# Reading the stationary operands of two attention products 128 columns wide instead of 99

## The chip, the cores and the metric

The kernel runs on one core of one Trainium2 chip. The metric is device time in microseconds (us). Each run also leaves a profile of one execution, the trace. The engines are named as in the profile: PE is TensorE's matmuls, PEld its weight loads (which overlap matmuls), DVE is VectorE, ACT is ScalarE, POOL is GpSimd and SP is SyncE.

## The reference

A layer norm with modulation, an attention block with 8 memory tokens and segments of 32 tokens, and an MLP, on 2048 tokens of width 1024. The part that matters is the attention of 32 heads of 128:

```python
q = jnp.einsum('btd,dhe->bhte', h, Wq)      # and k, v
scores = jnp.einsum('bhqe,bhke->bhqk', q, k) * scale
scores = jnp.where(mask[None, None], scores, -1000000000.0)
p = _softmax(scores, axis=-1)
o = jnp.einsum('bhqk,bhke->bhqe', p, v)
```

## The kernel before

The kernel packs the tokens of a head into 22 tiles: tile 0 has T0 = 104 columns, the others TW = 99 (three segments of 32 and three memory columns). Queries and keys of a head lie transposed, 128 partitions by 2188 columns, tile after tile. A score matmul has the keys of one tile as stationary operand (`lhsT`) and its queries as moving operand (`rhs`). Five tiles (a group) share one PSUM tile, one exponential on ACT and one mask multiply on DVE. An output matmul has the exponentials E as stationary operand and the values with a column of ones as moving operand (129 columns). There are 32 x 22 = 704 of each kind. The program interleaves them with the projections of the next head pair (480 moving columns each).

```python
def col0(t):
    return 0 if t == 0 else T0 + (t - 1) * TW

def scores(h, g):
    QT, KTt = QTs[h % 3], KTs[h % 3]
    rows = T0 if g == 0 else TW
    o = 0
    ps = psS.tile([P, 512], F32, name="ps_s")
    for t in SG[g]:
        w = T0 if t == 0 else TW
        nc.tensor.matmul(ps[:rows, o:o + w], lhsT=KTt[:, col0(t):col0(t) + rows], rhs=QT[:, col0(t):col0(t) + w], start=True, stop=True)
        o += w
    E = ep.tile([P, 512], BF16, name="E")
    # ... exponential on ACT, mask multiply on DVE, both on [:rows, 0:o]

def outs(h, j):
    V, O = Vs[h % 2], Os[h % 2]
    ts = VG[j]                                   # three tiles
    n, rows = len(ts), T0 if j == 0 else TW
    ps = psO.tile([P, 3, DH + 1], F32, name="ps_o")
    for i, t in enumerate(ts):
        k = T0 if t == 0 else TW
        nc.tensor.matmul(ps[:rows, i, :], lhsT=state["e", h, t // 5][:k, col0(t) - col0(t // 5 * 5):col0(t) - col0(t // 5 * 5) + rows], rhs=V[:k, t, 0:DH + 1], start=True, stop=True)
    # ... reciprocal and scaling on DVE or ACT
```

Of the kernel before, what the change touches and what calls it, by code (L numbers as in the profile page):

```python
# [9 lines left out]
BF16 = mybir.dt.bfloat16  # L10
# [9 lines left out]
P = 128  # L20
S = 2048
D = 1024
KT = D // P
H = 32
DH = 128
# [23 lines left out]
QW = T0 + (NT - 1) * TW + 5  # L49
# [11 lines left out]
def kernel(ctx, tc, A_x, A_mem0, A_Wq, A_Wk, A_Wv, A_Wo, A_seg_len, B_x, B_w1, B_w2, B_w3, B_w4, c, w_mod, out,  # L61
           dbg=None, force_fallback=False, no_fallback=False):
    nc = tc.nc
# [103 lines left out]
    def first_pass(late_hook):  # L167
# [55 lines left out]
        LQ = ExitStack()  # L223
        qkp = LQ.enter_context(tc.tile_pool(name="up_qk", bufs=1))
        QTs = [qkp.tile([P, QW], BF16, name=f"QT{i}") for i in range(3)]
        KTs = [qkp.tile([P, QW], BF16, name=f"KT{i}") for i in range(3)]
        VTs = [qkp.tile([P, NT, P], BF16, name=f"VT{i}") for i in range(2)]
        for t in QTs + KTs:
            nc.gpsimd.memset(t[:, 0:64], 0.0)
            nc.gpsimd.memset(t[:, QW - 5:QW], 0.0)  # L230
        for t in VTs:
            nc.gpsimd.memset(t[:], 0.0)

# [152 lines left out]
        for half in range(2):  # L386
            for j in range(KT):
                for kt in range(KT):
                    nc.tensor.matmul(pm[:, half * KT + j:half * KT + j + 1], lhsT=wms[half * 2 + j // 4][:, kt, (j % 4) * P:(j % 4 + 1) * P], rhs=scT[:, kt:kt + 1],
                                     start=(kt == 0), stop=(kt == KT - 1))  # L390
# [121 lines left out]
        LA = ExitStack()  # L512
# [6 lines left out]
            nc.gpsimd.memset(t[96:P, :, :], 0.0)  # L519
            nc.gpsimd.memset(t[0:96, 0, :], 0.0)  # L520
        otp = LA.enter_context(tc.tile_pool(name="up_ot", bufs=2))
        ep = LA.enter_context(tc.tile_pool(name="up_e", bufs=5))
        psS = LA.enter_context(tc.tile_pool(name="up_psS", bufs=2, space=PSUM))
        psO = LA.enter_context(tc.tile_pool(name="up_psO", bufs=2, space=PSUM))
        LX = ExitStack()
# [3 lines left out]
        state = {}  # L529
# [3 lines left out]
        def col0(t):  # L533
            return 0 if t == 0 else T0 + (t - 1) * TW
# [155 lines left out]
        SG = [list(range(5 * g, min(5 * g + 5, NT))) for g in range(5)]  # L690
        VG = [list(range(3 * j, min(3 * j + 3, NT))) for j in range(8)]

        def scores(h, g):
            QT, KTt = QTs[h % 3], KTs[h % 3]
            rows = T0 if g == 0 else TW
            o = 0
            ps = psS.tile([P, 512], F32, name="ps_s")
            for t in SG[g]:
                w = T0 if t == 0 else TW
                nc.tensor.matmul(ps[:rows, o:o + w], lhsT=KTt[:, col0(t):col0(t) + rows], rhs=QT[:, col0(t):col0(t) + w], start=True, stop=True)  # L700
                o += w
            E = ep.tile([P, 512], BF16, name="E")
            state["e", h, g] = E
            nc.scalar.activation(E[:rows, 0:o], ps[:rows, 0:o], ACT.Exp, scale=DH ** -0.5)  # L704
            mk = maskA if g == 0 else maskB
            nc.vector.tensor_tensor(E[:rows, 0:o], E[:rows, 0:o], mk[:rows, 0:o], ALU.mult)  # L706

        def outs(h, j):
            assert ("v", h) in state, h
            V, O = Vs[h % 2], Os[h % 2]  # L710
            ts = VG[j]
            n, rows = len(ts), T0 if j == 0 else TW
            ps = psO.tile([P, 3, DH + 1], F32, name="ps_o")
            for i, t in enumerate(ts):
                k = T0 if t == 0 else TW
                nc.tensor.matmul(ps[:rows, i, :], lhsT=state["e", h, t // 5][:k, col0(t) - col0(t // 5 * 5):col0(t) - col0(t // 5 * 5) + rows], rhs=V[:k, t, 0:DH + 1], start=True, stop=True)  # L716
            rin = rin_all[:rows, h, ts[0]:ts[0] + n]
            nc.vector.reciprocal(rin, ps[:rows, 0:n, DH])  # L718
            if j % 3 == 2:
                for i, t in enumerate(ts):  # L720
                    nc.scalar.mul(O[:rows, t, :], ps[:rows, i, 0:DH], rin[:, i:i + 1])
            else:
                nc.vector.tensor_tensor(O[:rows, ts[0]:ts[0] + n, :], ps[:rows, 0:n, 0:DH], rin[:, :, None].to_broadcast([rows, n, DH]), ALU.mult)  # L723
            if j == 7:
                state["outs", h] = True
# [37 lines left out]
        def attention():  # L763


            units = []
            tail = []
            waiting = []
            for h in range(H):
                for g in range(5):  # L770
                    units.append(lambda h=h, g=g: scores(h, g))
                    while waiting and waiting[0][0] <= 5 * h + g - 1:
                        units.append(waiting.pop(0)[1])
                    for j in range(8):
                        if VG[j][-1] // 5 == g:
                            waiting.append((5 * h + g, lambda h=h, j=j: outs(h, j)))
                            if h >= H - 2:
                                if j in (3, 6):
                                    waiting.append((5 * h + g, lambda h=h, j=j: turn(h, j // 3 - 1)))
                                elif j == 7:  # L780
                                    waiting.append((5 * h + g + 1, lambda h=h, j=j: turn(h, 2)))
                                    waiting.append((5 * h + g + 1, lambda h=h: keep(h)))
                            elif j == 7:
                                waiting.append((5 * h + g, lambda h=h: flip(h)))
                                waiting.append((5 * h + g + 3, lambda h=h: keep(h)))
                                if h % 2 and h + 2 < H:
                                    waiting.append((5 * h + g + 2, lambda h=h: to_v(h + 2)))
                    waiting.sort(key=lambda w: w[0])
            return units + [u for _, u in waiting]
# [547 lines left out]
    def general_pass():  # L1337
# [301 lines left out]
        def A_groups(hp, pool_norm=False):  # L1639

            def mk(hl, gi, tiles):
# [4 lines left out]
                def a():  # L1646
# [8 lines left out]
                    nc.vector.tensor_reduce(nmx[:TS, :nb], smk[:TS, :nb, :], AX.X, ALU.max, negate=True)  # L1655
                    E = sp.tile([P, GB, TS], F32, name='E')
                    ssum = sml.tile([P, GB], F32, name='ssum')
                    for b in range(nb):
                        nc.scalar.activation(E[:TS, b, :], smk[:TS, b, :], ACT.Exp, bias=nmx[:TS, b:b + 1], scale=1.0, accum_out=ssum[:TS, b:b + 1])
                    g['E'], g['ssum'] = (E, ssum)  # L1660

# [314 lines left out]

    cond_box = []
    first_pass(None if no_fallback else (lambda: cond_box.append(load_flag())))
    if no_fallback:
        return  # L1980
# [51 lines left out]
```

## Time and profile before

| | before |
|---|---|
| median of the first 3 runs | 1498.55 us (1498.49 to 1499.06) |
| PE busy, whole span | 1428.8 us, 95% |
| PE busy, attention stage 122 to 806 us | 669.8 of 684.0 us |
| first score matmul to first output-projection matmul | 660.50 us |

The page's first part gives busy time, share of the span and number of instructions of each engine:

```profile
PE 1428.8 (95%) x9118; PEld 761.0 (51%) x9118; DVE 931.4 (62%) x1965; ACT 666.3 (45%) x1407; POOL 360.3 (24%) x490
```

The windows view of the attention stage (start:end, length, then the busy time of each engine, then granted clock, DMA share and GB/s) shows that PE is hardly ever idle there, at full clock:

```profile
122.00:806.00 684.00, 669.80 (x4939) 401.63 (x4937) 472.96 (x1235) 414.90 (x988) 58.48 (x150) 1.00 0.77 177
```

The groups of weight loads by form (line, engine, operation, operand, partitions*columns, count; busy us, mean ns; idle time before them) show the target of the change. L716 and L700 are the output and score matmuls. Loads of 128 columns take 98 ns, those of 99 or 104 columns 126 to 128:

```profile
L716 PEld LDWEIGHTS <-E 99*99 99x99 bf16 x608 | 58.4, 126 | 29.4 <-issue 2.1 <-DVE E L706 2.0 <-DVE O L723 0.3
L700 PEld LDWEIGHTS <-KT 128*99 128x99 bf16 x544 | 43.4, 127 | 16.8 <-issue 1.0
L608 PEld LDWEIGHTS <-wq 128*128 128x128 bf16 x464 | 42.4, 98 | 36.1 <-issue 0.4
...
L754 PEld LDWEIGHTS <-O 96*128 96x128 bf16 x44 | 2.7, 98 | 0.9
```

The timeline of PE gives start and length of runs of equal instructions. Matmuls overlap, and their ends are modelled, so lengths are not costs. The cost is the step from start to start: a row's start is taken from the next row's. Five score matmuls at 482.82 take 0.23 us, 47 ns each; three output matmuls take 0.18. The first row and the one at 782.56 bound the attention interval (122.06 to 782.56, 660.50 us); the last two show waits for a DMA just after it:

```profile
122.06 0.64 PE L700 MATMUL ps_s<-QT,KT 128*104 128x104 bf16 x10
...
482.82 0.40 PE L700 MATMUL ps_s<-QT,KT 128*99 128x99 bf16 x5
483.05 0.37 PE L608 MATMUL acc<-hh,wv 128*128 128x480 bf16 x1
...
489.30 0.34 PE L716 MATMUL ps_o<-V,E 99*99 99x129 bf16 x3
489.48 0.37 PE L608 MATMUL acc<-hh,T 128*128 128x480 f16 x1
...
782.56 0.59 PE L877 MATMUL acc<-pre_w,pre_o 128*128 128x512 bf16 x2 [0.18 <-issue]
...
796.55 3.59 PE L877 MATMUL acc<-wstream,OTc 128*128 128x512 bf16 x8 [4.83 <-DMA OTc<-OTx_d]
...
818.09 1.25 PE L877 MATMUL acc<-wstream,pre_o 128*128 128x512 bf16 x4 [4.03 <-DMA wstream<-in_A_Wo_dram]
```

### The profile page before, as it was taken

To read this page: it belongs to the slowest core of one execution; us is meant where nothing else is said; L and a number is where in the kernel's file an instruction comes from. 1 tells how busy PE (TensorE), PEld (TensorE's weight loads), DVE (VectorE), ACT (ScalarE), POOL (GpSimd) and SP (SyncE) were. 2 spreads that over 40 slices of the span, in tenths; PEclk is the share of its full clock that TensorE was granted. 3 is DMA by queue.
4 is the path that set the end of the run, shared out by engine and by line. 5 is a ranking of instruction groups with operands and counts; after the bars stand their busy time and mean duration, and the time that the engine had idled before them with its cause. 6 is when DMAs were issued, how large, how long until landed. Compare 5 with 4: busy or idle time off the path is not lost.

```text
span 1496.1 us, 24409 instructions
## 1 busy us (share of the span) xinstructions
PE 1428.8 (95%) x9118; PEld 761.0 (51%) x9118; DVE 931.4 (62%) x1965; ACT 666.3 (45%) x1407; POOL 360.3 (24%) x490
## 2 busy tenths in 40 slices
PE   6699999999999999999997999999997999999997
PEld 3365656565556566665553444444443444444443
DVE  5726767677676777766651354354296667667684
ACT  2715666665665665666551031123434661046400
POOL 7502100000000000000110232213012563546525
PEclk9999999999999999999998999999999999999999
DMA  9576968876778877778579899994399774477712
GB/s 319 188 282 144 190 158 190 183 161 166 166 170 178 190 158 174 162 166 186 115 193 328 285 320 347 325 238 148 101 306 234 244 250 139 134 240 254 265 39 77
DMA packets 402611, 303.46 MB, mean 203 GB/s; under 512 B 199082, under 2 KB 354730, under 8 KB 400690
## 3 DMA queue, kind: packets, MB, share of 16 engines
q1 hardware_dynamic: 363632, 238.05, 60.4%
q0 software_dynamic: 9616, 33.05, 7.4%
q10 hardware_dynamic: 29234, 30.71, 6.7%
q8 instruction: 73, 1.20, 0.4%
q14 instruction: 56, 0.46, 0.1%
HBM read 200.56 MB, written 50.63 MB: 168 GB/s over the span
## 4 chain that ended last, share of the span: by engine, by line
PE 79%; DMA 6%; DVE 5%; issue 4%; ACT 3%; POOL 3%; ACTq 0%; SPq 0%; DVEq 0%; POOLq 0%
PE acc L608 31%; PE acc L877 7%; PE bank_b L1241 6%; PE bank_b L1190 6%; PE acc L1034 4%; PE acc L1117 3%; PE acc L328 3%; PE bank_d L1190 3%; PE bank_d L1241 2%; PE bank_e L1241 2%; PE ps_o L716 2%; DMA wstream<-in_A_Wo_dram 2%; PE ps_s L700 2%; PE acc L318 2%; DMA V<-VT 2%
## 5 line engine op out<-in xcount | busy, mean ns | idle before, releaser
L877 PE MATMUL acc<-wstream,OTc 128*128 128x512 bf16 x960 | 211.1, 382 | 5.3 <-DMA OTc<-OTx_d 4.8
L608 PEld LDWEIGHTS <-T 128*128 128x128 f16 x1408 | 130.8, 98 | 118.9 <-issue 1.7
L576 ACT COPY snap<-acc 128x480 f32<-128x480 f32 x264 | 146.3, 565 | 86.1 <-PE acc L608 79.5
L608 PE MATMUL acc<-hh,T 128*128 128x480 bf16 (+1 forms) x704 | 163.1, 366 | 0.3 <-DVE VT L580 0.3
L608 PE MATMUL acc<-hs,T 128*128 128x480 f16 x704 | 157.1, 366 | 0.6 <-ACT snap L576 0.6
L877 PEld LDWEIGHTS <-OTc 128*128 128x128 bf16 x960 | 94.0, 98 | 118.4 <-DMA OTc<-OTx_d 5.0
L1190 PEld LDWEIGHTS <-ring 128*128 128x128 f16 (+1 forms) x784 | 77.4, 99 | 108.2 <-issue 15.9
L744 POOL DMA_DIRECT2D OTx_d<-OT x32 | 24.8, 776 | 430.4 <-DMA OT<-O 318.8
L704 ACT ACTIVATE E<-ps_s 99x495 bf16<-99x495 f32 (+2 forms) x160 | 87.4, 547 | 48.2 <-PE ps_s L700 47.8
L608 PE MATMUL acc<-hh,wq 128*128 128x480 bf16 x464 | 103.9, 366 | 0.0
L723 DVE TENSOR_TENSOR O<-ps_o,rin_all 99x384 bf16<-99x384 f32 (+1 forms) x192 | 97.0, 509 | 3.8
L1060 DVE TENSOR_TENSOR ring<-ring 128x1024 f16<-128x1024 bf16 (+1 forms) x64 | 85.7, 1359 | 5.8 <-PE bank_b L1241 5.4
L1241 PEld LDWEIGHTS <-hq 128*128 128x128 bf16 (+1 forms) x560 | 54.9, 98 | 66.0
L580 DVE TENSOR_TENSOR KT<-acc,snap 128x480 bf16<-128x480 f32 x116 | 74.9, 654 | 21.4 <-PE acc L608 18.9
L716 PEld LDWEIGHTS <-E 99*99 99x99 bf16 (+2 forms) x704 | 67.7, 126 | 39.4 <-issue 5.4
L1155 ACT COPY snap<-bank_b 128x512 f32<-128x512 f32 x72 | 40.6, 583 | 102.8 <-PE bank_b L1241 60.7
L716 PE MATMUL ps_o<-V,E 99*99 99x129 bf16 (+2 forms) x704 | 80.5, 221 | 5.9 <-DMA V<-VT 4.3
L706 DVE TENSOR_TENSOR E<-E,maskB 99x495 bf16<-99x495 bf16 (+1 forms) x128 | 48.1, 376 | 48.6 <-ACT E L704 46.7
L110 POOL TENSOR_TENSOR ln_rstd<-ln_ve,mhalf 128x1 f32<-128x1 f32 x64 | 35.3, 552 | 172.8 <-DVE ln_ve L108 127.5
L975 ACT ACTIVATE u<-x,ln_nmr,ln_rstd 128x1024 bf16<-128x1024 f32 x16 | 19.7, 1232 | 126.3 <-DVE ln_nmr L974 124.1
L718 DVE RECIPROCAL rin_all<-ps_o 99x3 f32<-99x3 f32 (+2 forms) x256 | 42.7, 171 | 50.9 <-PE ps_o L716 50.0
L580 DVE TENSOR_TENSOR VT<-acc,snap 128x480 bf16<-128x480 f32 x90 | 58.0, 651 | 25.0 <-PE acc L608 21.0
(228 smaller groups left out, 2582.3 us busy)
## 6 DMA issues: line engine op xcount, KB each, us to landing
wstream<-in_A_Wo_dram SPq DMA_DIRECT2D x29, 1024.0 KB, 9.5
OTx_d<-OT POOLq DMA_DIRECT2D x32, 512.0 KB, 7.2
wstream<-in_B_w_dram SPq DMA_DIRECT2D x28, 512.0 KB, 5.4
ring<-in_B_w_dram SPq DMA_DIRECT2D x28, 512.0 KB, 6.2
ring<-in_B_w_dram SPq DMA_DIRECT2D x8, 1792.0 KB, 10.2
OTc<-OTx_d SPq DMA_DIRECT2D x12, 1024.0 KB, 7.2
wq<-in_A_Wq_dram SPq DMA_DIRECT2D x16, 512.0 KB, 6.0
wk<-in_A_Wk_dram SPq DMA_DIRECT2D x16, 512.0 KB, 8.7
```

What stands on the lines that cost most here:

```text
L576: nc.scalar.copy(t[:], st[q][bank][:, 0:CH])
L580: nc.vector.tensor_tensor(view(d, i), chunks(st[q][bank]), chunks(st[q][s_]), ALU.add)
L608: nc.tensor.matmul(acc[:, 0:CH], lhsT=B[:, k, :], rhs=A[:, k, :], start=(j in (1, 2, 5) and k == 0), stop=(k == 3), skip_group_check=True)
L704: nc.scalar.activation(E[:rows, 0:o], ps[:rows, 0:o], ACT.Exp, scale=DH ** -0.5)
L706: nc.vector.tensor_tensor(E[:rows, 0:o], E[:rows, 0:o], mk[:rows, 0:o], ALU.mult)
L716: nc.tensor.matmul(ps[:rows, i, :], lhsT=state["e", h, t // 5][:k, col0(t) - col0(t // 5 * 5):col0(t) - col0(t // 5 * 5) + rows], rhs=V[:k ...
L723: nc.vector.tensor_tensor(O[:rows, ts[0]:ts[0] + n, :], ps[:rows, 0:n, 0:DH], rin[:, :, None].to_broadcast([rows, n, DH]), ALU.mult)
L877: nc.tensor.matmul(accs[tt][:], lhsT=ot[hl // 4][:, hl % 4, tt * P:(tt + 1) * P], rhs=woc[hl // 4][:, hl % 4, :], start=(h == 0), stop=(h ...
L1034: nc.tensor.matmul(acc[:], lhsT=w1s[:, kt, ct * P:(ct + 1) * P], rhs=zT[:, kt, b * 512:(b + 1) * 512], start=(kt == 0), stop=(kt == KT - 1))
L1060: return nc.vector.tensor_tensor(dst, a, b, op)
L1190: nc.tensor.matmul(acc[:], lhsT=B[:, k, q * P:(q + 1) * P], rhs=A[:, k, :], start=(start and k == 0), stop=(k == 3), skip_group_check=True)
L1241: nc.tensor.matmul(acc[:], lhsT=L3[:, k, i * P:(i + 1) * P], rhs=R3[:, k, :], start=(start and k == 0), stop=(k == 13), skip_group_check=True)
```

## The change

The intent is to make the 1,408 weight loads of the attention products 128 columns wide, so that they go the way of the fast loads. The Trainium skill, "TensorE: Matmul & The Clock Gate", section "Weight-path perf modes — Fast Weight Load (FWL) and DoubleRow", states that the fast load is on when there are 128 weights and the type is not FP32. The loads read past their tile into the next one; the extra rows of the product are written to PSUM and never read. Keys get 24 spare columns, and E becomes five fixed tiles, cleared once, so that columns past the end are defined.

```diff
-        KTs = [qkp.tile([P, QW], BF16, name=f"KT{i}") for i in range(3)]
+        KTs = [qkp.tile([P, QW + 24], BF16, name=f"KT{i}") for i in range(3)]
...
-            nc.gpsimd.memset(t[:, QW - 5:QW], 0.0)
+            nc.gpsimd.memset(t[:, QW - 5:], 0.0)
...
-        ep = LA.enter_context(tc.tile_pool(name="up_e", bufs=5))
+        ep = LA.enter_context(tc.tile_pool(name="up_e", bufs=1))
+        Es = [ep.tile([P, 532], BF16, name=f"E{i}") for i in range(5)]
+        for t in Es:
+            nc.gpsimd.memset(t[:], 0.0)
...
-                nc.tensor.matmul(ps[:rows, o:o + w], lhsT=KTt[:, col0(t):col0(t) + rows], rhs=QT[:, col0(t):col0(t) + w], start=True, stop=True)
+                nc.tensor.matmul(ps[:, o:o + w], lhsT=KTt[:, col0(t):col0(t) + P], rhs=QT[:, col0(t):col0(t) + w], start=True, stop=True)
...
-            E = ep.tile([P, 512], BF16, name="E")
+            E = Es[(5 * h + g) % 5]
...
-                nc.tensor.matmul(ps[:rows, i, :], lhsT=state["e", h, t // 5][:k, col0(t) - col0(t // 5 * 5):col0(t) - col0(t // 5 * 5) + rows], rhs=V[:k, t, 0:DH + 1], start=True, stop=True)
+                c = col0(t) - col0(t // 5 * 5)
+                nc.tensor.matmul(ps[:, i, :], lhsT=state["e", h, t // 5][:k, c:c + P], rhs=V[:k, t, 0:DH + 1], start=True, stop=True)
```

## The prediction

> **What bounds the kernel.** The page gives PE 95% of the span busy, DVE 62%, ACT 45%, and the chain of waits 79% PE. The change acts in the attention stage, 122 to 806 us: there the windows view has PE busy 669.8 of 684.0 us at a granted clock of 1.00, weight loads (PEld) 401.6. So the stage is bound by the rate at which PE takes matmuls: by the step from one matmul's start to the next, not the modelled durations.
>
> **Costs now.** The groups by form show every 128-column weight load at 98 ns (also with only 96 partitions), and only the loads of 99 or 104 columns at 126 to 128 ns: 704 of keys (L700), 704 of exponentials (L716). This agrees with the Trainium skill, "TensorE: Matmul & The Clock Gate", section "Weight-path perf modes": a fast weight load is on when there are 128 weights not in FP32. The intent: bring 1,408 loads from 127 to 98 ns, 41 us summed.
>
> Loads overlap matmuls, so little of that is on the critical path. The same page, "Back-to-back issue gap", gives N/2.4 + 2.5 ns per matmul; the trace agrees: 480 columns start every 202 to 203 ns, 199 every 86, 96 (transposes of O, 128-wide stationary) every 42. By that rule 99 columns should step in 43.8 ns and 129 in 56.2. In the timeline five score matmuls take 0.23 to 0.24 us, 47 to 48 ns each; of three output matmuls the first step is 61 ns, the others 56. Summed over the stage, the excess over the rule is about 2.1 us after score matmuls and 1.1 us between output matmuls, 3.3 us in all: all that a faster load can take away. The stage's other 25 us of excess are 92 pauses of 20 ns or more, waits for E, V, snap and a DMA, which a load does not shorten.
>
> **Removed, added, moved.** Removed: 29 ns per load, of which about 3 ns per score matmul and 1.6 per output matmul show. Added: five clears of E on POOL (0.5 us each, estimated from 2.44 us for 2816 columns of O; POOL is free after 122.8 us, the first exponential starts at 124.0), and 24 columns in three clears of K. Matmuls write 128 partitions of PSUM instead of 99; the moving length, which sets the step, is unchanged. Moved: nothing. Instruction by instruction, each engine has the same order and, but for some start-up waits, the same waits. Fixed E tiles are reused at the same distance of five.
>
> **On the critical path.** At most 3.3 us; perhaps 0.5 remains as a start-of-group effect, and some is given back where PE then waits longer for DVE's masked E or a DMA. Expected gain 2.5 us of 1498.55, 0.2%.
>
> **Predicted: 1496.0 us, 1493.2 to 1498.6 (8 in 10). Faster by over 2%: 0.01; within 2%: 0.985; slower by over 2%: 0.005.**
>
> **What would show it.** Right: L700 and L716 loads at 98 ns; PEld busy down 20 to 40 us; five scores in 0.22 us, three outputs in 0.17; PE busy down a few us; the span down 2 to 3 us. Wrong: loads still near 127 ns; or 98 ns with the step unchanged (the excess is not the load's); or the step shorter and PE's idle time longer by as much.
>
> **What would make it wrong.** A slow load delaying more than its own group; a hidden cost of full-width PSUM writes; new waits, because a score matmul now also reads 29 columns of the next tile's keys and an output matmul some of its exponentials; shifted DMA collisions at 786 to 818 us, where the chain runs through a 32 us load of output weights.

## The result, and the profile after

| | before | after |
|---|---|---|
| median | 1498.52 us (1496.82 to 1499.06, 4 runs) | 1498.24 us (1496.43 to 1498.81, 4 runs) |
| ratio | | 0.9998, 95% interval 0.9981 to 1.0015 |
| first score to first output-projection matmul | 660.50 us | 659.70 us |

A ratio is worked out from fast runs of the same rounds, so it is not quite the ratio of the medians. The medians differ by 0.3 us, and the runs of one kernel by more than 2 us. Time alone cannot tell whether the change did anything; the trace can.

The page after:

```profile
PE 1425.5 (95%) x9118; PEld 750.9 (50%) x9118; DVE 924.3 (62%) x1965; ACT 665.5 (45%) x1407; POOL 359.1 (24%) x495
```

The windows view of the same stretch:

```profile
122.00:806.00 684.00, 670.89 (x4945) 392.75 (x4944) 472.95 (x1235) 413.19 (x985) 60.44 (x153) 1.00 0.77 178
```

The groups of weight loads by form. Every load of the attention products (L705 scores, L722 outputs) now takes 98 ns, so the trigger is shown:

```profile
L722 PEld LDWEIGHTS <-E 99*128 99x128 bf16 x672 | 53.6, 98 | 38.3 <-issue 4.9 <-DVE E L711 2.3 <-DVE O L729 0.3
L705 PEld LDWEIGHTS <-KT 128*128 128x128 bf16 x704 | 47.2, 98 | 23.8 <-issue 1.5
```

The timeline of PE, for the same matmuls as before. The five scores still take 0.23 us (481.09 to 481.32) and the three outputs 0.18. The interval is 120.74 to 780.44. After it PE waits for the same two DMAs, less for the first and more for the second:

```profile
120.74 0.62 PE L705 MATMUL ps_s<-QT,KT 128*128 128x104 bf16 x10
...
481.09 0.39 PE L705 MATMUL ps_s<-QT,KT 128*128 128x99 bf16 x5
481.32 0.36 PE L611 MATMUL acc<-hh,wv 128*128 128x480 bf16 x1
...
487.57 0.34 PE L722 MATMUL ps_o<-V,E 99*128 99x129 bf16 x3
487.75 0.37 PE L611 MATMUL acc<-hh,T 128*128 128x480 f16 x1
...
780.44 0.59 PE L883 MATMUL acc<-pre_w,pre_o 128*128 128x512 bf16 x2 [0.21 <-issue]
...
792.82 3.33 PE L883 MATMUL acc<-wstream,OTc 128*128 128x512 bf16 x8 [3.23 <-DMA OTc<-OTx_d]
...
815.13 4.45 PE L883 MATMUL acc<-wstream,pre_o 128*128 128x512 bf16 x10 [5.88 <-DMA wstream<-in_A_Wo_dram]
```

So the loads became 29 ns shorter and most steps hardly changed. The profiled run after began its attention 1.3 us earlier (120.74 against 122.06), which is before any changed matmul; other runs of either kind below start it between 121.2 and 122.2. That part of the shorter profiled span is therefore no gain of the change.

Summing over the stage each step minus (N/2.4 + 2.5 ns), N the moving columns, and leaving out pauses of 20 ns or more, the small excess fell from 4.31 to 3.50 us. The prediction had put 3.3 us of those 4.31 down to the loads and expected about 2.8 of them (3.3 less 0.5) to go before anything was given back. What, then, makes up the rest, if not the loads?

This sum has a blind spot. A step that falls below the limit of 20 ns leaves the pauses and enters the sum. In the attention interval 74 steps were pauses before and 59 after; those 15 steps became 0.44 us shorter in all, which the sum does not show. They return under keys_only.

### The profile page after: what moved, and what is told of

It reads as the page before. It is cut to its first block, busy times and chain, and to the rows that moved or that the text cites. A ratio compares the mean times of both kernels' runs of the same rounds, so it can differ in the third digit from the quotient of the medians.

```text
span 1494.7 us, 24413 instructions
## 1 busy us (share of the span) xinstructions
PE 1425.5 (95%) x9118; PEld 750.9 (50%) x9118; DVE 924.3 (62%) x1965; ACT 665.5 (45%) x1407; POOL 359.1 (24%) x495
## 4 chain that ended last, share of the span: by engine, by line
PE 79%; DMA 7%; DVE 5%; issue 3%; ACT 3%; POOL 2%; SPq 0%; ACTq 0%; DVEq 0%; POOLq 0%
PE acc L611 31%; PE acc L883 7%; PE bank_b L1247 6%; PE bank_b L1196 6%; PE acc L1040 4%; PE acc L1123 3%; PE acc L328 3%; PE bank_d L1196 3%; PE bank_d L1247 2%; PE bank_e L1247 2%; PE ps_o L722 2%; DMA wstream<-in_A_Wo_dram 2%; PE acc L318 2%; PE ps_s L705 2%; DMA V<-VT 2%
## 5 line engine op out<-in xcount | busy, mean ns | idle before, releaser
L722 PE MATMUL ps_o<-V,E 99*128 99x129 bf16 (+1 forms) x704 | 79.5, 220 | 6.2 <-DMA V<-VT 4.3
L1066 DVE TENSOR_TENSOR ring<-ring 128x1024 f16<-128x1024 bf16 (+1 forms) x64 | 78.5, 1248 | 5.6 <-PE bank_b L1247 5.2
L722 PEld LDWEIGHTS <-E 99*128 99x128 bf16 (+1 forms) x704 | 56.2, 98 | 43.7 <-issue 4.9
L1247 PE MATMUL bank_b<-ring,hq 128*128 128x512 f16 (+1 forms) x336 | 73.2, 379 | 0.0
```

The lines of the kernel that those rows point to most:

```text
L722: nc.tensor.matmul(ps[:, i, :], lhsT=state["e", h, t // 5][:k, c:c + P], rhs=V[:k, t, 0:DH + 1], start=True, stop=True)
L1066: return nc.vector.tensor_tensor(dst, a, b, op)
L1247: nc.tensor.matmul(acc[:], lhsT=L3[:, k, i * P:(i + 1) * P], rhs=R3[:, k, :], start=(start and k == 0), stop=(k == 13), skip_group_check=True)
```

## The experiments

The single starts in the trace gave a hint. Sorted by tile, the median steps in ns of the score matmuls in the second group of a head, and of its first output triple after tile 0's (tiles 3 to 5), are:

| kernel | scores, tiles 5 to 9 | outputs, tiles 3 to 5 |
|---|---|---|
| before | 44, 48, 47, 48, 46 | 61, 56, 56 |
| after | 44, 48, 47, 47, 43 | 61, 56, 56 |

Only tile 9 gained clearly (and likewise 1 and 17). Their queries and keys begin at columns 104, 896 and 1688, which are the only multiples of 8 besides tile 0. The first output matmul of a triple comes after a projection over 128 partitions and is itself over 99. Hence the rivals. Theory L is the one that was predicted from: the excess is the load. Theory B says that it comes from where the moving operand begins, and from a change in the number of partitions. C blames the start of the stationary operand, D the place in PSUM. All variants below start from the changed kernel and gave correct results; the runs without rounds are one run each, whose times (1495.5 to 1499.2 us, the two with bursts apart) decide nothing and are not compared. The evidence is in the steps and in the interval.

### bursts: the load and the step measured by themselves

```diff
+        def burst(h, ps):
+            rows, kc, kw, qc, n, o = BURST[h]
+            for r in range(40):
+                k = rows or (128, 99)[r % 2]
+                nc.tensor.matmul(ps[:kw, o:o + n], lhsT=KTs[h % 3][:k, kc:kc + kw], rhs=QTs[h % 3][:k, qc:qc + n], start=True, stop=True)
...
             ps = psS.tile([P, 512], F32, name="ps_s")
+            if g == 1 and h in BURST:
+                burst(h, ps)
```

> The changed kernel with 22 extra bursts of 40 matmuls each, one in each of heads 2 to 23, into a score tile that the real score matmuls overwrite; they measure by themselves the start-to-start step against the width of the stationary operand, where the two operands begin, the moving length and the number of partitions. Theory L (the one predicted from: the excess over N/2.4 + 2.5 ns is the slow weight load): with 32 moving columns the step is set by the load, about 45 ns for 99 columns and below 30 for 128, with 127 and 64 columns as slow per column as 99; with 99 moving columns and fast loads 44 ns wherever the queries begin. Theory B (the excess is of the moving operand's start and of a change in the number of partitions): loads as in L, but with 99 moving columns, fast loads and queries from column 203 the step is 47 ns against 44 from column 64; from columns 72 and 80 (multiples of 8) it is 44, from 68 and 65 47; 129 columns from 203 are also 3 to 4 ns slower; a burst alternating 128 and 99 partitions is 3 to 5 ns a step slower than one with 99 throughout. Theory C (the start of the stationary operand): keys from column 203 are slow wherever the queries begin. Theory D (place in PSUM): queries from 64 written from column 99 of the tile are 3 to 4 ns slower.

The timeline of PE in this kernel, bursts of 40. A row's length is 39 steps and one modelled matmul. With 32 moving columns and 128, 99, 127 and 64 stationary ones:

```profile
156.93 1.17 PE L711 MATMUL ps_s<-QT,KT 128*128 128x32 bf16 x40
...
181.05 2.03 PE L711 MATMUL ps_s<-QT,KT 128*99 128x32 bf16 x40
...
202.94 2.54 PE L711 MATMUL ps_s<-QT,KT 128*127 128x32 bf16 x40
...
227.97 1.44 PE L711 MATMUL ps_s<-QT,KT 128*64 128x32 bf16 x40
...
497.34 2.43 PE L711 MATMUL ps_s<-QT,KT 99*128 99x129 bf16 x40
...
521.58 2.53 PE L711 MATMUL ps_s<-QT,KT 128*128 128x129 bf16 x40
```

From first to last start, the mean steps are 25.4 ns for 128 columns, 47.0 for 99, 59.7 for 127 and 32.2 for 64. One column short of 128 costs 34 ns a step, if nothing hides it. This is the number that the prediction lacked: **a 99-wide load needs 47 ns of step.** With 99 moving columns the 99-wide load made the step 47.4 ns, with queries from column 64 and from 203 alike. In a steady stream an output matmul steps in 56 ns or more anyway, which covers it; a score matmul steps in 47 to 48 anyway in most tiles.

The last two rows are 129 moving columns over 99 partitions throughout (56.7 ns a step), and in turn over 128 and 99 (59.1 ns; the row's operand is that of its first matmul). A change in the number of partitions costs time, as B said, though 2.4 ns a step and not the 3 to 5 expected. The start of the queries did not do what B said: with the same operands 40 times over and 99 moving columns, the step was 44.2 ns with queries from columns 64, 68, 72 and 80, and only 45.0 from 65 and 203. Keys from 203 gave 44.2, so C falls; another place in PSUM gave 44.2, so D falls. That half of B was missed, or it needs something that a fixed burst does not have.

### keys_only: only half of the change

```diff
-                nc.tensor.matmul(ps[:, i, :], lhsT=state["e", h, t // 5][:k, c:c + P], rhs=V[:k, t, 0:DH + 1], start=True, stop=True)
+                nc.tensor.matmul(ps[:rows, i, :], lhsT=state["e", h, t // 5][:k, c:c + rows], rhs=V[:k, t, 0:DH + 1], start=True, stop=True)
```

> Only the keys are read 128 wide; exponentials again 99 or 104 wide. Theory L: output matmuls go back to the excess of the kernel before and half of the gain goes with it. Theory B: the steps between output matmuls (61, 56, 56 ns) are the same with loads of 98 and of 127 ns, because 129 moving columns cover both; so key loads at 98 ns, exponential loads at 126 ns, and the small excess of the attention stage within 0.2 us of the 3.5 us of the change, nearly all of its 0.8 us kept.

The exponentials' loads are back at 125 ns, the median output steps are still 61, 56, 56, and the small excess of the stage is 3.55 us against 3.50, as theory B expected. But the interval is 660.01 us: of the 0.8 us only 0.5 was kept, not nearly all.

Set side by side matmul by matmul, the traces of keys_only and of the changed kernel show what the medians hide. Eleven output steps are 27 to 31 ns longer in keys_only, the whole difference of the loads. Each belongs to the first output matmul after a pause of PE of 60 ns or more, and its own load had started only 1 to 5 ns before it (the median is 59 ns), so that the next load could not be hidden either. Fourteen more, each after a run of projection matmuls of 71 columns, are 9 to 12 ns longer. One of the eleven, first in keys_only (510.12 to 510.33, 0.21 us), then in the changed kernel (0.18 us):

```profile
510.12 0.37 PE L722 MATMUL ps_o<-V,E 99*99 99x129 bf16 x3
510.33 0.39 PE L705 MATMUL ps_s<-QT,KT 128*128 128x99 bf16 x5
...
508.73 0.34 PE L722 MATMUL ps_o<-V,E 99*128 99x129 bf16 x3
508.91 0.39 PE L705 MATMUL ps_s<-QT,KT 128*128 128x99 bf16 x5
```

All output steps together are 0.53 us longer. In the interval 0.31 of that shows against the trace of the changed kernel and 0.53 against its second trace (659.48, below). So the shorter loads of the exponentials are worth about 0.5 us, not in the usual triple, but where the loads had no time to run ahead. The small excess misses the eleven, because with the slow load they count as pauses.

### rows128: no change in the number of partitions

The rows beyond 99 or 104 are zeros in E (cleared, masked) and in V, so that the output matmul may run over all 128.

```diff
-                nc.tensor.matmul(ps[:, i, :], lhsT=state["e", h, t // 5][:k, c:c + P], rhs=V[:k, t, 0:DH + 1], start=True, stop=True)
+                nc.tensor.matmul(ps[:, i, :], lhsT=state["e", h, t // 5][:, c:c + P], rhs=V[:, t, 0:DH + 1], start=True, stop=True)
```

> The changed kernel with the output matmuls contracted over all 128 partitions, the rows beyond 99 or 104 being zeros in both operands, so that every matmul of the stage has the same number of partitions. Theory B: the first step of each group of output matmuls falls from 61 to 56 ns, some 1 us less in the stage. Theory L, or a cost of the place in PSUM: it stays at 61.

The timeline of PE, the same triple: 0.17 us instead of 0.18.

```profile
488.29 0.33 PE L722 MATMUL ps_o<-V,E 128*128 128x129 bf16 x3
488.46 0.37 PE L611 MATMUL acc<-hh,T 128*128 128x480 f16 x1
```

Sorted by tile, every output step is now 56 to 57 ns, the first of a triple too. The small excess of the stage fell to 2.54 us, and the interval to 658.99. So the 61 ns, which the prediction booked to the load, were the price of going from 128 partitions to 99: 0.7 us of the interval.

### q_grid: queries on a grid of 8 columns

```diff
+QP = 104
+QQ = T0 + (NT - 1) * QP
...
-        QTs = [qkp.tile([P, QW], BF16, name=f"QT{i}") for i in range(3)]
+        QTs = [qkp.tile([P, QQ], BF16, name=f"QT{i}") for i in range(3)]
...
-        Es = [ep.tile([P, 532], BF16, name=f"E{i}") for i in range(5)]
+        Es = [ep.tile([P, 532 if i < 4 else 228], BF16, name=f"E{i}") for i in range(5)]
...
-                nc.tensor.matmul(ps[:, o:o + w], lhsT=KTt[:, col0(t):col0(t) + P], rhs=QT[:, col0(t):col0(t) + w], start=True, stop=True)
+                nc.tensor.matmul(ps[:, o:o + w], lhsT=KTt[:, col0(t):col0(t) + P], rhs=QT[:, qcol(t):qcol(t) + w], start=True, stop=True)
```

(`qcol(t)` is `T0 + (t - 1) * QP`, and the projections write queries with that pitch. The shorter last E only makes room.)

> The changed kernel with tiles of queries every 104 columns instead of every 99, so that each moving operand of a score matmul begins at a multiple of 8 columns; keys stay every 99. Theory B: all score steps at 43 to 44 ns instead of 44 to 48, some 1.4 to 1.7 us less in the stage. Theory C (start of the keys) and D (place in PSUM): steps stay at 47 in all but 4 to 7 of 22 tiles.

The timeline of PE, the same five scores: 0.22 us.

```profile
481.55 0.38 PE L711 MATMUL ps_s<-QT,KT 128*128 128x99 bf16 x5
481.77 0.37 PE L617 MATMUL acc<-hh,wv 128*128 128x480 bf16 x1
```

Every score step is 44 ns (46 for tile 0 with its 104 columns), as N/2.4 + 2.5 has it. The interval is 658.72 us, 1.0 us less, where 1.4 to 1.7 were expected: the score steps gave 1.4 us, but steps of projection matmuls took 0.3 us of it back, and why is open. So the start of the queries does matter in the real sequence, though not in a fixed burst. Two explanations were left: both operands off the grid at once (E), or a moving operand off the grid that begins elsewhere each time (F).

### bursts2 and k_grid: which of the two

The second set of bursts takes lists of columns in turn; `WALK` is the kernel's own sequence of tile starts. `k_grid` gives the pitch of 104 to the keys instead of the queries (and clears the five spare columns of each tile).

```diff
+        WALK = [T0 + i * TW for i in range(20)]
+                k, q, o = kc[r % len(kc)], qc[r % len(qc)], r % 5 * TW * walk
+                nc.tensor.matmul(ps[:kw, o:o + TW], lhsT=KTs[h % 3][:, k:k + kw], rhs=QTs[h % 3][:, q:q + TW], start=True, stop=True)
```

> The first bursts gave 44.2 ns for 99 columns with a 128-wide load on the 8-column grid, 45.0 with queries from column 203 alone, 44.2 with keys from 203 alone: neither start explains the 47 to 48 ns of the real score matmuls. Here both operands are off the grid, or they change from one matmul to the next as in the kernel. Theory E (both off the grid at once): both fixed at 203 takes 47 ns, queries fixed at 203 with walking keys 47, and walking queries over fixed keys from 64 only 45. Theory F (a moving operand that begins elsewhere each time, off the grid): walking queries over fixed keys take 47, both fixed at 203 only 45, two queries in turn at 203 and 302 take 47, at 64 and 168 44. Both: both walking takes 47 to 48 but 44 in the tiles whose queries begin on the grid; with the place in PSUM walking too it is the same; 99-wide loads with both walking take 47 to 48 throughout.

> The changed kernel with tiles of keys every 104 columns, so that each stationary operand of a score matmul begins on the 8-column grid; queries stay every 99. Theory E (both off the grid at once): score steps fall to 44 to 45 ns, as with queries on the grid. Theory F (walking moving operand off the grid): unchanged, 47 to 48 in all but the group-first and the three on-grid tiles.

The timeline of PE in the kernel with the second bursts. First walking queries over fixed keys, then walking keys under fixed queries from column 64, then both fixed at 203:

```profile
156.82 2.03 PE L710 MATMUL ps_s<-QT,KT 128*128 128x99 bf16 x40
...
181.79 1.93 PE L710 MATMUL ps_s<-QT,KT 128*128 128x99 bf16 x40
...
228.00 1.96 PE L710 MATMUL ps_s<-QT,KT 128*128 128x99 bf16 x40
```

| stationary from | moving from | mean step, ns |
|---|---|---|
| 64 | walking | 46.7 |
| walking | 64 | 44.2 |
| 203 | 203 | 45.0 |
| walking | 203 | 45.0 |
| walking | walking | 46.7 |
| 64 | 203 and 302 in turn | 45.0 (43 and 47 in turn) |
| 64 | 203 and 64 in turn | 44.6 (44 and 45 in turn) |
| 64 | 64 and 168 in turn | 44.2 |
| walking, 99 wide | walking | 47.1 |

Walking queries alone are slow, off-grid operands standing still are not, and within the walk the steps of the on-grid tiles are 43 to 44 as in the kernel. So E falls, and F holds for this walk. In k_grid the score steps stayed at 44, 48, 48, 47, 43 and the interval at 659.51 us: the stationary operand's start costs nothing. A multiple of 4 is not enough: tile 13 begins at column 1292 and steps in 47 ns.

As it was stated, F is too wide: 203 and 302 in turn should have taken 47 ns and took 45.0. The single steps suggest a narrower rule. The slow step, 47, is always that of 302, where the operand before it (203 to 301) ended. The step of 203 is 43 after 302 and 44 after 64. In the kernel the first score of a group, which follows a projection and not the neighbouring queries, takes 44 in tiles 5, 10, 15 and 20, all off the grid; tiles 9 and 17, on the grid right behind their neighbours, take 43. All of this fits: slow when the moving operand begins off the grid and just where the one before it ended. q_grid removed both conditions at once, and no run tested queries off the grid with gaps between them, so the narrower rule is read from the traces and not proved. What in the hardware pays is open.

### q_grid_narrow: the loads' worth where nothing hides them

Queries on the grid, and both loads 99 or 104 wide again.

```diff
-                nc.tensor.matmul(ps[:, o:o + w], lhsT=KTt[:, col0(t):col0(t) + P], rhs=QT[:, qcol(t):qcol(t) + w], start=True, stop=True)
+                nc.tensor.matmul(ps[:rows, o:o + w], lhsT=KTt[:, col0(t):col0(t) + rows], rhs=QT[:, qcol(t):qcol(t) + w], start=True, stop=True)
-                nc.tensor.matmul(ps[:, i, :], lhsT=state["e", h, t // 5][:k, c:c + P], rhs=V[:k, t, 0:DH + 1], start=True, stop=True)
+                nc.tensor.matmul(ps[:rows, i, :], lhsT=state["e", h, t // 5][:k, c:c + rows], rhs=V[:k, t, 0:DH + 1], start=True, stop=True)
```

> Queries on the grid, but both stationary operands again 99 or 104 wide. The bursts gave 47 ns for a 99-wide load by itself and at most 25 for a 128-wide one. So the score steps should be 46 to 48 ns in every tile, set by the load; output steps as in both kernels (61, 56, 56). The interval from the first score matmul to the first output-projection matmul should be some 2 us longer than the 658.7 us with queries on the grid and wide loads: there the wide load is worth its predicted 2 us, while it was worth 0.8 us with queries off the grid. If it is 658.7 too, the load is not what sets the step of 46 to 48.

Score steps are 44, 47, 47, 47, 47 in the second group: 47 as expected, but not in the first of a group. With the other runs this makes a two-by-two table of the interval in us:

| | loads 99 wide | loads 128 wide | worth of the wide load |
|---|---|---|---|
| queries every 99 columns | 660.50 | 659.70 | 0.80 |
| queries on the grid | 660.53 | 658.72 | 1.81 |

The grid alone is worth nothing (660.50 to 660.53), the wide load alone 0.8 us, both together 1.8. Two limits of about 47 ns lie on top of each other in the score steps, and removing one leaves the other: the mean score step within a group is 47.3 ns before and 46.3 with the wide load alone, 47.0 with the grid alone and 44.4 with both. Some 0.4 to 0.5 us of either worth are the output steps of keys_only, which the grid does not touch.

One wait within the interval blurs it. An output matmul waits for masked exponentials, and DVE in its turn for weights (wk) that a DMA brings. In all nine traces without bursts this matmul starts 2.62 us after DVE goes on, but 13.91 to 14.35 us after the first score matmul, as the transfer lands. Counted from this matmul on, the table's first row reads 646.56 and 645.60 us, its second 646.61 and 644.68, and the wide load is worth 0.96 and 1.94 us (0.99 in the second trace of the change).

### after_again and q_grid_rows128: timed

The changed kernel itself, and the changed kernel with the edits of q_grid and rows128 together, each in five rounds beside the kernel before.

> The changed kernel itself, timed in five rounds beside the kernel before. From the traces, the change shortens the way from the first score matmul to the first output-projection matmul by 0.8 us (660.50 to 659.70), and nothing else in it. So the interval from first score to first output-projection matmul should again be 659.7 us within 0.2, and the median 0.5 to 1.5 us below that of the kernel before, which is inside a spread from run to run of some 2 us; the theory predicted from (a slow load costs 2.5 us) would give 2 to 3 us.

> Wide loads, queries on the 8-column grid and output matmuls over all 128 partitions together: the three terms that the traces gave add to 660.50 minus 0.8 (wide loads alone) minus 1.0 (grid) minus 0.7 (no change of partitions) = 658.0 us from the first score to the first output-projection matmul, with score steps at 44 and output steps at 56 to 57 ns. The median should be 2 to 3 us (0.15 to 0.2%) below that of the kernel before. If the interval is 658.0 and the median is not lower, later waits for the output weights take the gain back.

| | median, us | ratio to before | 95% interval | interval first score to output projection |
|---|---|---|---|---|
| before | 1497.53 (1496.17 to 1499.03, 9 runs) | | | 660.50 |
| after_again | 1497.36 (1494.19 to 1498.77, 5 runs) | 1.0003 | 0.9989 to 1.0017 | 659.48 |
| q_grid_rows128 | 1495.53 (1492.96 to 1497.97, 5 runs) | 0.9989 | 0.9976 to 1.0003 | 658.21 |

In the traces the expectations were nearly met. The change's interval is 659.48 us, 0.02 outside the margin; the other is 658.21 where 658.0 was expected, with score steps at 44 and output steps at 57 ns. In time the change was again not to be seen: its median was 0.2 us lower, short of the 0.5 to 1.5 us expected, and the ratio is 1.0003. The version with all three edits has a median 2.0 us lower, of the size expected, but its interval just includes 1. It is not proved to be faster.

Why time says so little: the other stretches vary by more from run to run than any of this. From the first output-projection matmul to the first matmul of the MLP's first layer, a stretch that begins with the two DMA waits shown above, the nine traces (before, after and seven others without bursts, after_again included) took 237.3 to 241.0 us, in no order that goes with the edits: 239.9 before, 239.6 after, 238.1 after_again, 241.0 q_grid, 237.3 q_grid_narrow, 239.5 q_grid_rows128. I found no sign that this stretch takes a gain back systematically, and this number of runs cannot rule it out for less than a microsecond.

## Why the prediction was right or wrong

- **The time was right.** 1498.24 us lies within 1493.2 to 1498.6, and "within 2%" was right. That supports nothing: the unchanged kernel's 1498.52 us lies in the range too. The range had to be wide for noise, and with an effect of this size being inside it was luck as much as insight.
- **What bounds the stage was right:** PE, by its steps. So was the warning that 41 us of shorter loads are almost all hidden.
- **The trigger was right:** 128 columns load in 98 ns. Summed singly the loads fell by 41 us (938.4 to 897.0), as reckoned. PEld busy fell by 10 us (761.0 to 750.9), not 20 to 40: busy time counts overlapping loads once, and the prediction allowed for too little of that.
- **The failed step** is "3.3 us in all: all that a faster load can take away", with "about 3 ns per score matmul and 1.6 per output matmul", and from it the "expected gain 2.5 us". The excess over N/2.4 + 2.5 was measured rightly, but all of it was put down to the load because the load was the slow thing in sight. The term measured 0.8 us in the interval (1.0 in the second trace). For scores it is about 0.9 ns on average within a group instead of 3 (47.3 to 46.3), because off-grid queries hold most steps at 47 to 48 by themselves. For outputs it is 0.5 us instead of 1.1, and not where it was booked: the 61 ns are the change from 128 to 99 partitions, and the usual triple gained nothing.
- **A second step failed beside it:** the pauses of 20 ns or more, "which a load does not shorten". Fifteen of them did become shorter, by some 29 ns each (11 after output and 4 after score matmuls), because right after a wait the loads had no lead (1 to 5 ns over their matmul). These 0.44 us are close to half of what the change gained.
- **A sign was there to be read.** The prediction noted "the first step is 61 ns, the others 56" for three equal loads. Equal loads alone do not explain unequal steps.
- **The feared costs did not come.** PSUM writes of 128 partitions, five clears and the reads across tiles left no new wait of PE in the trace; the one for masked exponentials near 136 us that grew goes with the landing of wk, as told above.

## What to carry to other kernels

Before pricing a slow load, measure by a short burst what step it enforces by itself, and compare that with the step that the matmuls have anyway; only the difference can be gained. Look apart at the matmuls right after a wait: there a load has no lead and shows in full, and a cut-off that calls such steps pauses hides it. When two limits of nearly the same size lie on one step, removing either gives little and removing both gives more than the sum of the two, so test them in a two-by-two. Below about 0.2% of a run, the step and the interval in the trace decide more than the clock does.

## What the Trainium skill lacked or had wrong

- "TensorE: Matmul & The Clock Gate", section "LDWEIGHTS (loading the stationary operand)", gives the number of columns over 1.2 in ns, which is 82.5 ns for 99 columns. At a granted clock of 1.00 the step that the load enforces was 32.2 ns for 64 columns, 47.0 for 99 and 59.7 for 127, about 0.44 ns a column and 4 ns; the recorded lengths of single loads were 113, 128 and 140 ns.
- The same page, section "Weight-path perf modes", gives about 2 times for the fast load. Here 128 columns stepped in 25.4 ns and 127 in 59.7, at least 2.35 times; the section "Wait — 56ns, not 53.3ns?" gives a floor of about 25 ns between starts, so the fast load itself may be shorter still.
- The same page, section "Back-to-back issue gap", gives N/2.4 + 2.5 ns for the isolated gap, and that held here (44.2 ns for 99, 202.5 for 480). For a real stream of loads and matmuls it gives about 81 ns for 128 columns and 131 for 512 instead; here such streams stepped in 56 to 57 ns for 129 columns and in 216 for 512 (40 matmuls from 805.27 us in the trace before). No page says that a moving operand that begins off a grid of 8 bf16 columns made the step 46 to 49 ns for 99 columns in the kernel's walk of tile starts, where each begins where the one before ended.
- No page says what a slow load costs right after a wait. Here it was the whole difference: 11 output steps were 27 to 31 ns shorter with loads of 98 instead of 125 ns.
- No page has the cost of a change in the number of partitions between neighbouring matmuls: 61 instead of 56 to 57 ns for the first matmul over 99 after one over 128, and 59.1 instead of 56.7 on average when they take turns.
